# RWKV-5 attention and channel mixing on one core: decay weights as one row, second weight matrix in one burst, and a new order of the start

## The chip, the cores and the metric

The kernel runs on one core of one Trainium2 chip. The metric is the device time of one execution in microseconds (us). A profile is one execution recorded by the hardware profiler; its span runs from the first to the last instruction. Engines are named as in the profile: PE is TensorE (PEld its weight loads), DVE is VectorE, ACT is ScalarE, POOL is GpSimd, SP is SyncE, which here only issues DMAs.

## The reference

Inputs `r`, `k`, `v` have shape (4, 8, 768, 48): batch, heads, tokens, head dimension. Each head carries a 48x48 state through the tokens; the channel mixing that follows works on all 384 channels of a token.

```python
for t in range(S):
    cur = einsum('bhd,bhe->bhde', u[None] * kt, vt)
    y[:, :, t] = einsum('bhd,bhde->bhe', rt, state + cur)
    state = w[None, :, :, None] * state + einsum('bhd,bhe->bhde', kt, vt)
...
x = y.transpose(0, 2, 1, 3).reshape(4, 768, 384)
xn = (x - mean(x)) / sqrt(var(x) + 1e-06) * g_ln
out = x + maximum(xn @ w_ch1, 0.0) @ w_ch2      # w_ch1 (384, 1536), w_ch2 (1536, 384)
```

The term with `u` is the current-token term: for each token and head it is a number, the sum over the head dimension of r·u·k, times v.

## The kernel before

The tokens of each batch are cut into 6 chunks of 128, which makes 24 chunks, numbered 0 to 23; chunks 0, 6, 12 and 18 start with an empty state. Inside a chunk the recurrence is written as matrix products. With the position p of a token in its chunk, r is multiplied by w^p (step `SR`, giving `scr`) and k by w^-(p+1) (`SK`, giving `sck`); the factors `Fr` and `Fk` are made once, as exponentials of the logarithm of w (`LN`, `FR`, `FK`). Then, per chunk i:

- `LK`, `LR`, `LV` load k, r, v (192 KB each, in pieces of 192 bytes; ten buffers each). `CV` casts v to bf16.
- `TR` transposes scr and sck on PE into PSUM, `TC` (or its halves `TCr`, `TCk`) copies them out to `trs`. For chunks of the list K_BY_DMA two DMA transposes on SP do this instead (`TRD`, `TKD`).
- `AT` multiplies the transposed k and r into scores, `AM` masks them on DVE. `S` makes the chunk's addition to the state; `ZU` and `ZD` make the decayed state `Z` of it. `Y` is masked scores times v, plus r times the state of the chunk before.
- The current-token number per head is `cc`. For most early chunks it is made on PE: `Q` multiplies the transposed r and k, four small matmuls inside `S` sum them with u·w, and `CC` copies the result out. For chunks of the list CC_BY_DVE, `KU` and `KR` multiply k by u·w and by r, and `CC` is a sum on DVE. `VB` on POOL is v times cc.
- `X` adds Y and VB and gives the sum for the mean; `SQ` the squares; `XN` centres the row; `RS` makes the inverse deviation.

Channel mixing runs over groups of one or two chunks (GROUPS). `LT` and `XT` (or the DMA transpose `LTD`) transpose xn; `UP` is the product with w_ch1 into one of two PSUM banks named `hp`, twelve matmuls for a group of one chunk, six of double width for a group of two; `RL` is the relu out of `hp` into `hT`; `DN`, three steps of four matmuls per chunk, is the product with w_ch2; `OT` scales it, adds x, and `STO` stores. `UP,16*g+m` is part m of group g; `DN,4*i+d` is part d of chunk i.

The weight w_ch1 is loaded in three blocks of 768 KB each on SP (`LW1,n`) and cast to bf16 with the factor -g_ln in nine steps (`SW,3n` to `SW,3n+2`; `g_neg`). For a group of one chunk, UP part m needs block n = m. The weight w_ch2 is loaded in three blocks by DMAs that POOL issues and that cast to bf16 on the way (`IW2`; the page calls the queue q0, software_dynamic). `WU` and `DU` are matmuls of zeros that keep PE busy.

Nothing is scheduled by a program at build time: PLAN lists the steps in order, each with an index and an engine (v DVE, s ACT, g POOL), and every engine executes its own in that order. So an instruction that waits holds back all that stands behind it on its engine. SP issues its loads and stores one after another, and a full queue holds SP.

Steps and lines used below: `WF` L219, `LN` L267, `CL` L286 and its helper L281, `UR` L295, `FK` L307, `FR` L310, `LW1` L330, `SW` L332, `IW2` L344, `LK` L347, `LR` L350, `LV` L353, `TR` L369, `AT` L403, `S` L429 with L434, L441 and L448, `Y` L481 and L489, `LTD`, `TKD`, `TRD` L524, L528, L532, `LT` L537, `UP` L552, `RL` L568 and L570, `DN` L580. L204, L206 and L209 are helpers for copies and products.

Of the kernel before, what the change touches and what calls it, by code (L numbers as in the profile page):

```python
# [10 lines left out]
ACT = mybir.ActivationFunctionType  # L11
ENG = mybir.EngineType

GROUPS = [1, 1, 1, 1, 1, 1, 2, 2, 2, 2, 2, 2, 2, 2, 1, 1]
ZPE = [1, 2, 3]
K_BY_DMA = [16, 17, 18, 19, 20, 21, 22, 23]
CC_BY_DVE = [10, 11, 12, 13, 14, 15, 16, 17, 18, 19, 20, 21, 22, 23]
W_ROWS = True
SLOTS = {'kf': 10, 'rf': 10, 'vf': 10, 'sck': 3, 'scr': 3, 'vv': 4, 'trs': 3, 'q': 2, 'A': 2, 'cc': 4, 'ku': 2, 'kr': 2, 'Z': 3, 'ZS': 2, 'Vb': 3, 'x': 13, 'xn': 3, 'xT': 4, 'hT': 4, 'ot': 3}
PLAN = """  # L20
MW,0,v WF,0,- TL,0,s MI,0,g MP,0,v WU,13,- MM,0,g LK,0,- LN,0,s LR,0,- RI,0,s DU,10,-
CL,0,- FR,0,s LW1,2,- FK,0,s SR,0,v SK,0,v DU,12,- TR,0,- WL,0,s LR,1,- LV,0,- UR,0,g
LK,1,- TCk,0,s DU,18,- CU,0,- SR,1,g CV,0,s TCr,0,v LK,2,- SK,1,v AT,0,- LR,2,- UW,0,s
Q,0,v UGC,0,s TR,1,- SW,6,s SW,8,v LV,1,- SW,7,v S,0,- AMa,0,v CC,0,s LV,2,- TCk,1,s
SK,2,g AMb,0,v TCr,1,s LW1,0,- DU,16,- Y,0,- CV,1,s ZU,0,v CV,2,s SR,2,g DU,6,- AT,1,-
Q,1,v VB,0,g DU,5,- TR,2,- AMa,1,v S,1,- TC,2,s AMb,1,v IW2,0,g LW1,1,- IW2,1,g X,0,v
CC,1,s SW,1,s Q,2,v DU,13,- AT,2,- IW2,2,g XN,0,v Y,1,- SW,0,s AM,2,v SW,2,g LT,0,-
SQ,0,s LR,3,- XT,0,v VB,1,g ZU,1,v DU,15,- UP,2,- X,1,v S,2,- RL,2,s SW,3,v SW,5,v
XN,1,s DU,1,- UP,0,- CC,2,v SR,3,v SW,4,s VB,2,g LT,1,- LK,3,- DU,1,- Y,2,- RL,0,s
UP,1,- XT,1,s RS,0,g LV,3,- ZU,2,v UP,18,- SK,3,v SQ,1,s LR,4,- DN,0,- RL,1,s X,2,v  # L30
TR,3,- RS,1,g LK,4,- RL,18,s UP,16,- TC,3,v XN,2,s CV,3,v AT,3,- RL,16,s Q,3,v UP,17,-
SR,4,v SQ,2,s SK,4,g AM,3,v LT,2,- S,3,- RS,2,g LK,5,- XT,2,v Y,3,- TR,4,- CC,3,v
RL,17,s LV,4,- UP,32,- VB,3,g TC,4,s DN,1,- LR,5,- X,3,v RL,32,s UP,34,- Q,4,v XN,3,s
LK,6,- SK,5,v AT,4,- ZU,3,v RL,34,s LT,3,- UP,33,- AM,4,v XT,3,s SQ,3,s CV,4,g UP,50,-
RL,33,s SR,5,v RS,3,g S,4,- RL,50,s Y,4,- CC,4,v TR,5,- ZU,4,v LR,6,- VB,4,g UP,48,-
TC,5,s SK,6,v DN,2,- ZD,4,g LV,6,- X,4,v AT,5,- OT,0,v LV,5,- UP,49,- SQ,4,s Q,5,v
XN,4,s DN,4,- SR,6,v RS,4,g LK,7,- RL,49,s LT,4,- S,5,- DN,5,- XT,4,s CC,5,v LUB,0,-
CV,6,g AM,5,v TR,6,- CV,5,g LR,7,- DN,6,- RL,48,s VB,5,g LK,8,- Y,5,- SK,7,v TC,6,s
UP,64,- UWR,0,g X,5,v LV,12,- UP,66,- XN,5,s Q,6,v SR,7,g AT,6,- RL,64,s LV,7,- OT,1,v
LT,5,- SQ,5,s S,6,- DN,8,- XT,5,v SK,8,g LR,9,- CC,6,v AM,6,v RL,66,s TR,7,- RS,5,g  # L40
UP,81,- LR,8,- ZU,6,v UP,80,- VB,6,g TC,7,v LR,10,- DN,9,- RL,81,s SR,9,g Q,7,v LK,9,-
AT,7,- CV,7,s Y,6,- SR,8,g DN,10,- RL,80,s X,6,v LV,8,- UP,82,- OT,2,v SQ,6,s LK,10,-
S,7,- AM,7,v XN,6,s SR,10,g DN,12,- CC,7,s RL,82,s LR,12,- LT,6,- DN,13,- VB,7,g ZU,7,v
CV,8,s XT,6,v Y,7,- STO,0,- ZD,7,g TR,8,- LK,11,- X,7,v DN,14,- SK,10,g TC,8,v XN,7,s
UP,65,- LV,10,- Q,8,v SK,9,g LT,7,- AT,8,- RL,65,s LK,12,- XT,7,v S,8,- KU,10,v SQ,7,s
UP,96,- SK,11,g OT,3,v LV,9,- CC,8,s TR,9,- AM,8,v UP,101,- VB,8,g TC,9,s LR,11,- DN,16,-
ZU,8,v RS,6,g RL,96,s STO,1,- Y,8,- Q,9,v CV,9,s DN,17,- ZD,8,g LK,16,- X,8,v CV,12,s
S,9,- RL,101,s KR,10,v AT,9,- LK,14,- CC,9,s XN,8,s SK,12,v TR,10,- VB,9,g SQ,8,s AM,9,v
UP,99,- LR,20,- TC,10,s DN,18,- SR,11,g ZU,9,v LV,11,- UP,97,- CV,10,s CC,10,v ZD,9,g RL,99,s
AT,10,- OT,4,v STO,2,- RL,97,s S,10,- KU,12,v LT,8,- LK,13,- DN,20,- XT,8,s ZU,10,v SR,12,g  # L50
CV,11,s Y,9,- AM,10,v STO,3,- DN,21,- VB,10,g LV,13,- TR,11,- X,9,v ZD,10,g DN,22,- TC,11,s
LR,13,- KU,11,v Y,10,- SK,13,g UP,100,- OT,5,v SQ,9,s LK,15,- KR,11,v AT,11,- XN,9,s DN,24,-
LR,15,- SK,14,v RL,100,s KU,13,g X,10,v LT,9,- UP,98,- LR,16,- XT,9,s SR,13,v CV,13,s S,12,-
TR,12,- CC,11,v RL,98,s LV,14,- UP,114,- AM,11,v RS,7,g TC,12,s UP,117,- LK,21,- VB,11,g ZU,12,v
SQ,10,s Y,11,- KR,13,v TR,13,- LR,14,- XN,10,g X,11,v RL,114,s AT,12,- KR,12,v S,13,- RL,117,s
STO,5,- SK,15,v UP,112,- TC,13,s AM,12,v STO,4,- UP,113,- LK,19,- XN,11,s DN,25,- SK,16,g KU,14,v
RL,112,s LR,22,- LT,10,- DN,26,- XT,10,s SR,16,v UP,115,- LK,22,- SQ,11,s SR,14,v OT,6,v Y,12,-
RL,113,s TR,14,- RS,8,g LK,18,- CC,12,v RL,115,s DN,28,- TC,14,s AT,13,- LK,17,- KU,15,v SR,15,v
DN,29,- VB,12,g ZU,13,v LR,17,- TR,15,- AM,13,v UP,116,- ZD,13,g TC,15,s LV,15,- DN,30,- X,12,v
CV,14,g RL,116,s AT,14,- LR,23,- CC,13,v SQ,12,s Y,13,- OT,7,v LT,11,- STO,6,- S,14,- XN,12,g  # L60
DN,32,- XT,11,s KR,14,v LV,18,- VB,13,g LT,12,- KU,16,v UP,132,- TKD,16,- SK,17,g UP,131,- X,13,v
RL,132,s AM,14,v DN,33,- CV,15,s SR,17,g RL,131,s LV,16,- UP,130,- XN,13,s KR,15,v DN,34,- ZU,14,v
XT,12,s LR,18,- RL,130,s KU,17,v Y,14,- ZD,14,g OT,8,v S,15,- LR,19,- AT,15,- CV,18,v SQ,13,s
DN,36,- SK,18,g ZU,15,v STO,7,- UP,129,- CC,14,v LV,20,- ZD,15,g LT,13,- DN,37,- RL,129,v XT,13,s
LV,23,- UP,128,- KR,16,v SR,18,g AM,15,v DN,38,- TRD,16,- RL,128,s UP,133,- CV,16,s VB,14,g OT,9,v
S,16,- TRD,17,- KU,18,v UP,144,- RL,133,s RS,9,g ZU,16,v DN,40,- X,14,v SK,19,g LV,17,- CC,16,v
DN,41,- SQ,14,s UP,145,- SR,19,v LV,19,- DN,42,- CC,15,v VB,16,g RL,144,v XN,14,s LK,20,- Y,15,-
AT,16,- KR,18,v RL,145,s VB,15,g OT,10,v UP,147,- STO,8,- CV,19,s AM,16,v KR,17,g DN,44,- STO,9,-
UP,149,- CV,17,g X,15,v TKD,17,- ZD,16,g DN,45,- RL,147,v Y,16,- RL,149,v KU,19,g UP,148,- X,16,v
CV,20,s STO,10,- LT,14,- XN,15,s CC,18,v SR,20,g DN,46,- XT,14,v SQ,15,s LV,22,- RL,148,v AT,17,-  # L70
SQ,16,s S,18,- OT,11,v LT,15,- UP,146,- TKD,18,- SK,20,g CC,17,v XT,15,s DN,48,- RL,146,s RS,10,g
UP,163,- TKD,19,- AM,17,v DN,49,- VB,18,g RL,163,s UP,164,- ZU,18,v TRD,18,- XN,16,s VB,17,g KR,19,v
DN,50,- RL,164,s KU,20,g Y,17,- LK,23,- OT,12,v UP,160,- SK,21,g X,17,v DN,52,- TRD,19,- RL,160,s
KR,20,v AT,18,- KU,21,g CC,20,v DN,53,- LTD,16,- S,19,- SR,22,g DN,54,- AM,18,v XN,17,s UP,162,-
LR,21,- SQ,17,s SK,22,g OT,13,v UP,161,- RL,162,s CC,19,v AT,19,- KU,22,g LTD,17,- ZU,19,v UP,165,-
RL,161,s AM,19,v S,20,- RS,11,g DN,56,- TRD,20,- Y,18,- ZD,19,g RL,165,s UP,177,- X,18,v UP,181,-
TKD,20,- SR,21,g SQ,18,s Y,19,- RL,177,s DN,57,- VB,19,g KR,21,v STO,11,- UP,179,- SK,23,g STO,12,-
RL,181,s X,19,v DN,58,- ZU,20,v RL,179,s LV,21,- XN,18,g CC,21,v UP,180,- SQ,19,s SR,23,g TRD,21,-
XN,19,s UP,176,- OT,14,v RL,180,s AT,20,- CV,21,v RS,12,g DN,60,- LTD,18,- AM,20,v S,21,- DN,61,-
KU,23,g CV,23,v LTD,19,- Y,20,- ZD,20,g DN,62,- RL,176,v UP,178,- TKD,21,- OT,15,v VB,21,g UP,197,-  # L80
ZU,21,v VB,20,g RL,178,v DN,64,- TKD,22,- ZD,21,g AT,21,- X,20,v UP,193,- AM,21,v CV,22,g STO,13,-
SQ,20,s DN,65,- KR,23,g TRD,23,- RL,193,s S,22,- DN,66,- RL,197,s KR,22,g Y,21,- TRD,22,- UP,192,-
OT,16,v XN,20,g CC,22,v UP,194,- RL,192,s ZU,22,v VB,22,g STO,15,- DN,68,- X,21,v STO,14,- CC,23,v
AT,22,- SQ,21,s DN,69,- STO,16,- VB,23,g AM,22,v RL,194,s UP,195,- LTD,20,- RS,13,g XN,21,s DN,70,-
ZD,22,g UP,196,- TKD,23,- RL,195,s OT,17,v Y,22,- DN,72,- LTD,21,- AT,23,- X,22,v DN,73,- RL,196,s
XN,22,v STO,17,- SQ,22,s UP,210,- DN,74,- RS,14,g RL,210,s UP,212,- OT,18,v UP,209,- DN,76,- RL,212,s
LTD,22,- RL,209,s DN,77,- UP,208,- STO,18,- DN,78,- RL,208,s UP,211,- OT,19,v UP,213,- AM,23,v RL,211,s
DN,80,- RL,213,s DN,81,- STO,19,- DN,82,- Y,23,- OT,20,v UP,224,- DN,84,- X,23,v RL,224,s DN,85,-
XN,23,v STO,20,- DN,86,- SQ,23,s UP,226,- RS,15,g OT,21,v LTD,23,- UP,225,- RL,226,s DN,88,- RL,225,s
UP,240,- STO,21,- DN,89,- RL,240,s DN,90,- UP,241,- UP,242,- OT,22,v RL,241,s DA,0,- RL,242,s DA,1,-  # L90
DA,2,- DB,0,- STO,22,- OA,23,v DB,1,- DB,2,- OB,23,v SA,23,- SB,23,-
"""


@with_exitstack
def kernel(
    ctx: ExitStack,
    tc: tile.TileContext,
    r: bass.AP,
# [36 lines left out]
    group_of = {}  # L136
    for g, size in enumerate(GROUPS):
        for j in range(size):
# [545 lines left out]
```

## Time and profile before

| | |
|---|---|
| seven runs | median 156.38 us, 154.71 to 156.91 |
| the profiled execution | 156.68 us, span 154.6 us |
| PE busy | 144.2 us, 93% of the span |
| DVE, POOL, ACT busy | 110.1, 96.8, 89.0 us |
| mean granted PE clock | 0.975 |
| one UP step in the dense part, group of one / of two chunks | 0.67 / 0.655 us |
| one DN step (4 matmuls) | 0.65 us |
| AT / TR (scr and sck) / LT | 0.33 / 0.45 / 0.17 us |

The time of an execution is about 2.1 us longer than the span that its profile shows. Durations of the last three rows are distances between starts in the chain of work that ended last; single matmuls in the page's groups are longer, because matmuls overlap. A busy PE in the first 15 us is partly matmuls of zeros.

### The profile page before, as it was taken

Reading aid. Unit: us, or ns where it says so; the run is one execution under the profiler, and the core shown is the slowest. Engines: PE = TensorE matmul, PEld = TensorE weight load, DVE = VectorE, ACT = ScalarE, POOL = GpSimd, SP = SyncE. Lnnn points to the kernel's source line nnn. Section 1 sums busy time; section 2 is a strip of 40 time slices with the busy share of each in tenths; the row PEclk is TensorE's granted clock in tenths of the full one; section 3 lists DMA queues with packets and bytes.
Section 4 is the critical chain, followed back from the end, with each engine's and each line's share of the span. In section 5 each row is a group of like instructions: output and inputs, shape, how many; then the busy total and the mean of one; then the engine's idle time right before and its main releaser. Section 6 shows DMA issues by size and latency. Waiting matters only on the chain.

```text
span 154.6 us, 4487 instructions
## 1 busy us (share of the span) xinstructions
PE 144.2 (93%) x1788; PEld 117.3 (76%) x1788; DVE 110.1 (71%) x225; ACT 89.0 (58%) x186; POOL 96.8 (63%) x133
## 2 busy tenths in 40 slices
PE   7798975599999999999999999999999999999992
PEld 6697864488878788779877787777887777887881
DVE  2229950777989789999999789998877976335112
ACT  3536395148776658969966754376455147443440
POOL 3056636043799999998288598999899976100100
PEclk9999999559999999999999999999999999999998
DMA  4997999998999999989989978976472555212311
GB/s 70 288 233 137 303 260 207 199 194 167 183 184 203 205 220 193 246 171 211 244 162 223 227 149 193 230 77 139 100 203 53 134 156 140 77 55 79 99 55 51
DMA packets 92456, 25.98 MB, mean 168 GB/s; under 512 B 87442, under 2 KB 90900, under 8 KB 92436
## 3 DMA queue, kind: packets, MB, share of 16 engines
q1 hardware_dynamic: 92000, 24.52, 72.8%
q0 software_dynamic: 432, 1.18, 3.9%
q8 instruction: 14, 0.23, 0.6%
q14 instruction: 6, 0.05, 0.1%
q10 hardware_dynamic: 4, 0.00, 0.0%
HBM read 19.27 MB, written 4.72 MB: 155 GB/s over the span
## 4 chain that ended last, share of the span: by engine, by line
PE 79%; SPq 9%; DMA 9%; DVE 1%; issue 1%
PE hp L552 30%; PE o L580 29%; DMA rf<-in_r_dram 9%; PE at L403 5%; PE tr L369 4%; PE y L489 3%; SPq L353 3%; SPq L347 2%; PE s L448 2%; SPq L330 2%; PE y L481 2%; PE tr L537 2%; SPq L350 1%; PE o L595 1%; PE hp L595 1%
## 5 line engine op out<-in xcount | busy, mean ns | idle before, releaser
L552 PE MATMUL hp<-xT,w_sb 128*128 128x128 bf16 (+1 forms) x576 | 58.4, 250 | 0.3 <-DVE xT L206 0.2
L580 PE MATMUL o<-w_sb,hT 128*128 128x384 bf16 x276 | 55.0, 326 | 0.0
L552 PEld LDWEIGHTS <-w_sb 128*128 128x128 bf16 x576 | 49.1, 116 | 4.3 <-issue 0.5
L568 ACT ACTIVATE hT<-hp 128x512 bf16<-128x512 f32 x65 | 37.9, 595 | 22.4 <-PE hp L552 21.9
L580 PEld LDWEIGHTS <-hT 128*128 128x128 bf16 x276 | 24.8, 98 | 11.1 <-issue 0.2
L413 DVE TENSOR_TENSOR A<-at,mask 128x1024 bf16<-128x1024 f32 (+1 forms) x26 | 29.3, 1133 | 0.9 <-PE at L403 0.7
L636 DVE SCALAR_TENSOR_TENSOR ot<-o,rs,x 128x384 f32<-128x384 f32 x23 | 14.1, 612 | 16.2 <-PE o L580 14.5
L471 POOL TENSOR_TENSOR Vb<-vf,cc 128x384 f32<-128x384 f32 x24 | 21.1, 883 | 5.0 <-DVE cc L206 3.1
L209 POOL TENSOR_TENSOR sck<-kf,Fk 128x384 bf16<-128x384 f32 x15 | 16.1, 1080 | 11.3 <-PE at L403 6.0
L503 ACT ACTIVATE sqj<-x,sm 128x384 bf16<-128x384 f32 x24 | 14.7, 614 | 10.4 <-DVE x L496 10.3
L496 DVE SCALAR_TENSOR_TENSOR x<-y,Vb 128x384 f32<-128x384 f32 x24 | 13.2, 549 | 4.7 <-PE y L489 2.4
L204 ACT COPY trs<-tr 128x1024 bf16<-128x1024 bf16 (+1 forms) x14 | 12.8, 924 | 6.3 <-PE tr L369 6.3
L517 POOL TENSOR_SCALAR rs<-sq 128x1 f32<-128x1 f32 (+1 forms) x16 | 3.8, 236 | 18.6 <-ACT sqj L503 17.7
L209 POOL TENSOR_TENSOR scr<-rf,Fr 128x384 bf16<-128x384 f32 x14 | 14.6, 1047 | 0.8 <-DMA rf<-in_r_dram 0.8
L509 ACT ACTIVATE xn<-x,sm 128x384 bf16<-128x384 f32 x17 | 10.4, 613 | 6.5 <-DVE x L496 6.5
L209 POOL TENSOR_TENSOR Z<-ZS,WLZ 128x384 bf16<-128x384 f32 x13 | 13.4, 1032 | 1.1 <-DVE ZS L465 1.0
L209 DVE TENSOR_TENSOR scr<-rf,Fr 128x384 bf16<-128x384 f32 x10 | 5.7, 574 | 8.9 <-DMA rf<-in_r_dram 4.8
L262 PE MATMUL o<-warm 128*128 128x128 bf16 x110 | 10.6, 264 | 1.0 <-DVE warm L227 1.0
L204 ACT CAST vv<-vf 128x384 bf16<-128x384 f32 x14 | 7.1, 513 | 6.6 <-DMA vf<-in_v_dram 4.2
L520 POOL TENSOR_TENSOR rs<-rs,expo 128x1 f32<-128x1 f32 (+1 forms) x16 | 10.0, 625 | 1.3
L403 PE MATMUL at<-trs 48*128 48x128 bf16 x192 | 9.8, 222 | 0.1
L262 PEld LDWEIGHTS <-warm 128*128 128x128 bf16 x110 | 8.9, 122 | 1.1 <-DVE warm L227 1.0
(81 smaller groups left out, 190.0 us busy)
## 6 DMA issues: line engine op xcount, KB each, us to landing
kf<-in_k_dram SPq DMA_DIRECT2D x24, 192.0 KB, 4.1
rf<-in_r_dram SPq DMA_DIRECT2D x24, 192.0 KB, 4.3
vf<-in_v_dram SPq DMA_DIRECT2D x24, 192.0 KB, 4.1
out_dram<-ot SPq DMA_DIRECT2D x23, 192.0 KB, 2.8
w_f<-in_moe_w_ch_dram SPq DMA_DIRECT2D x3, 768.0 KB, 7.1
w_sb<-in_moe_w_ch_dram POOLq DMA_DIRECT2D x3, 384.0 KB, 8.8
w_b<-in_w_dram SPq DMA_DIRECT2D x1, 192.0 KB, 3.7
u_b<-in_u_dram SPq DMA_DIRECT2D x1, 192.0 KB, 4.5
```

What stands on the lines that cost most here:

```text
L204: nc.scalar.copy(out=out, in_=in_)
L209: engines[e].tensor_tensor(out=out, in0=in0, in1=in1, op=ALU.mult)
L262: nc.tensor.matmul(out=warm_ps[0][:, :P], lhsT=warm[:], rhs=warm[:], start=True, stop=True)
L403: nc.tensor.matmul(out=t[:, par, q, :], lhsT=trs(i)[p0 : p0 + D, 1, q, :], rhs=trs(i)[p0 : p0 + D, 0, q, :], start=True, stop=True,)
L413: nc.vector.tensor_tensor(out=AA(i)[:, a:b].rearrange("p e q t -> p (e q) t"), in0=psum["at", i][:, a:b].rearrange("p e q t -> p (e q) t") ...
L471: nc.gpsimd.tensor_tensor(out=Vb(i)[:].rearrange("p (h d) -> p h d", h=H), in0=vf(i)[:], in1=cc(i)[:].unsqueeze(2).to_broadcast([P, H, D]) ...
L496: nc.vector.scalar_tensor_tensor(out=xx(i)[:], in0=psum["y", i][:, :C], scalar=1.0, in1=Vb(i)[:], op0=ALU.mult, op1=ALU.add, accum_out=sm[ ...
L503: nc.scalar.activation(out=sqj[:], in_=xx(i)[:], func=ACT.Square, bias=sm[i][:], scale=-float(C), accum_out=sq[g][:, j : j + 1])
L552: nc.tensor.matmul(out=t[:, a * gw : (a + 1) * gw], lhsT=w1_sb[n][kc][:, fb::FB], rhs=xT(g)[:, kc, :gw], start=(kc == 0), stop=(kc == CK - 1),
L568: nc.scalar.activation(out=o, in_=s, func=ACT.Relu)
L580: nc.tensor.matmul(out=psum["o", i][:, :C], lhsT=hT(g)[:, fk, j * P : (j + 1) * P], rhs=w2_sb[d][:, a, :], start=(fk == 0), stop=(fk == FK ...
L636: nc.vector.scalar_tensor_tensor(out=ot(i)[:], in0=psum["o", i][:, :C], scalar=rs[g][:, j : j + 1], in1=xx(i)[:], op0=ALU.mult, op1=ALU.add,)
```

## The change

The functions stay as they are; five constants and PLAN are new.

```diff
-GROUPS = [1, 1, 1, 1, 1, 1, 2, 2, 2, 2, 2, 2, 2, 2, 1, 1]
+GROUPS = [1, 1, 1, 1, 1, 1, 1, 1, 2, 2, 2, 2, 2, 2, 2, 1, 1]
-K_BY_DMA = [16, 17, 18, 19, 20, 21, 22, 23]
-CC_BY_DVE = [10, 11, 12, 13, 14, 15, 16, 17, 18, 19, 20, 21, 22, 23]
-W_ROWS = True
+K_BY_DMA = [15, 16, 17, 18, 19, 20, 21, 22, 23]
+CC_BY_DVE = [12, 13, 14, 15, 16, 17, 18, 19, 20, 21, 22, 23]
+W_ROWS = False
```

With W_ROWS false, `WF` loads w as one row of 1.5 KB instead of 128 equal rows, `LN` takes the logarithm of one row, and a new step `WBM` spreads it to 128 rows by a matmul in float32 (1x128 ones by 1x384), from whose PSUM bank `FK` and `FR` read. The 128 rows of w that the current-token term on DVE needs come later by a new load, `LWB`.

```python
def WBM(i, e):
    t = psum["wb"] = ps.tile([P, 512], FP32, name="y")
    nc.tensor.matmul(out=t[:, :C], lhsT=ones[:], rhs=ln_b[:], start=True, stop=True)
def LWB(i, e):
    nc.sync.dma_start(out=w_b[:], in_=row_src(w, P))
```

PLAN is written anew throughout. The start of the SP queue, and what stands around the w_ch2 loads on POOL:

```diff
 SP
-WF LK0 LR0 LW1,2 LR1 LV0 LK1 LK2 LR2 LV1 LV2 LW1,0 LW1,1 LR3 LK3 LV3 LR4 LK4 LK5 LV4 LR5
+WF LK0 LR0 LR1 LK1 LV1 LV0 LK2 LR2 LV2 LR3 LW1,1 LK3 LW1,0 LR4 LV3 LK4 LW1,2 LV4 LK5 LR5
 POOL
-UR SR1 SK2 SR2 VB0 IW2,0 IW2,1 IW2,2 SW2 VB1
+UR SK1 SK2 VB0 SR2 SR3 XN0 IW2,0 IW2,1 IW2,2 VB1 RS0 XN1 SW2 VB2
 PE, behind S0 (matmuls of zeros: DU and how many)
-DU16 Y0 DU6 AT1 DU5 TR2 S1 DU13 AT2 Y1 LT0 DU15 UP2 S2 DU1 UP0 LT1 DU1 Y2 UP1 UP18 DN0 TR3
-UP16 AT3 UP17 LT2 S3 Y3 TR4 UP32
+DU16 AT1 DU5 Y0 S1 DU3 TR2 DU1 Y1 DU1 AT2 LT0 DU1 S2 DU9 UP1 TR3 DU3 Y2 DU6 LT1 DU3 AT3 DU3
+UP17 DU4 UP0 UP16 LT2 Y3 DN0 UP32 TR4 UP33 S3 UP34 UP2
 ACT, around SW8
+SW1 RL17 SQ2 RL0 XT2 SW8 RL32 RL33
 SP, near the end
-LTD19 TKD21 TKD22 STO13 TRD23 TRD22 STO15 STO14
+LTD19 STO13 STO14 TRD22 LK22 LR23 STO15 LTD20
```

The matmuls of zeros fall from 110 to 77. Several element-wise steps change engine: relu on ACT 65 to 69 and on DVE 7 to 3; XN on ACT 17 to 8, on POOL 4 to 10, on DVE 3 to 6; KR on DVE 11 to 5, on POOL 3 to 7; `Q` 10 to 12 times on DVE.

## The prediction, made before the changed kernel ran

> **What bounds the kernel now.** I read the page's busy shares and slices first, then the chain that ended last in order of time, the stretches of 2 us around the place that the chain points to, and the queues that act there.
>
> ```profile
> PE 144.2 (93%) x1788; PEld 117.3 (76%) x1788; DVE 110.1 (71%) x225; ACT 89.0 (58%) x186; POOL 96.8 (63%) x133
> ...
> PE   7798975599999999999999999999999999999992
> ...
> PEclk9999999559999999999999999999999999999998
> ```
>
> PE is full from the tenth slice on; no other engine is near that over the span. Two slices have half the clock. The chain says why:
>
> ```profile
> 14.22 0.49 SPq L330
> 14.75 13.19 DMA rf<-in_r_dram
> 27.96 0.56 DVE scr L209
> 28.52 0.23 DVE Z L209
> 28.91 0.56 DVE sck L209
> 29.51 0.61 PE tr L369 x4
> ```
>
> Until 14.7 us the chain is SP issuing loads, then r of chunk 3 (LR3, 13.19 us to landing), then PE to the end. The stretches (PE and PEld busy, DVE, ACT, POOL, granted clock, DMA share, GB/s):
>
> ```profile
> 18.00:20.00 2.00, 1.79 (x34) 1.67 (x30) 1.82 (x3) 0.57 (x1) 0.56 (x2) 1.00 0.99 371
> 22.00:24.00 2.00, 1.59 (x31) 1.52 (x32) 0.95 (x3) 2.00 (x5) 0.74 (x1) 1.00 1.09 204
> 26.00:28.00 2.00, 0.00 (x0) 0.00 (x0) 0.04 (x1) 0.00 (x0) 0.00 (x0) 0.87 1.16 228
> ```
>
> (28 to 34 us has a clock of 0.50.) And the issues, from the timeline of POOL and SP:
>
> ```profile
> 16.23 1.85 POOL L344 DMA_DIRECT2D w_sb<-in_moe_w_ch_dram  x3
> ```
>
> ```profile
> 13.43 1.27 SPq L330 DMA_DIRECT2D w_f<-in_moe_w_ch_dram  x2
> 14.75 0.49 SPq L350 DMA_DIRECT2D rf<-in_r_dram  x1
> 17.57 7.03 SPq L353 DMA_DIRECT2D vf<-in_v_dram  x1
> ```
>
> LR3 stands behind two w_ch1 blocks. These landed at 19.4 (ACT stopped waiting) and 14.2 + 8.0 = 22.2. The three w_ch2 pieces landed 7.6, 8.8 and 10.4 us after their issue: 23.9, 25.8, 27.9. r, k and v of chunk 3 landed at 27.95, 28.7, 29.5, only after the last of w_ch2. So while w_ch2 moves, about 5.8 us, the SP queue gets next to nothing through. PE stood 3.24 + 0.33 us for chunk 3, and the clock was halved from 27.4 to 34.3.
>
> **What the hole costs.** PE resumed at 28.58 and made its last matmul at 151.63. In the 5.7 us to 34.3 half was lost, 2.8 us. So from TR3 on there were 151.63 - 28.58 - 2.8 = 120.2 us of PE work at full clock, with no idle of note. The 3.0 us of store behind it stay. The change can win only ahead of this.
>
> **The change: the start of the SP queue.** It puts chunks 0 to 2 and LR3 ahead of any w_ch1. I walk it by rows. LK0, issued at about 1.2 us, lands after the shortest time of a chunk load, 2.9 us, plus a little: 4.4 (5.3 now, behind 192 KB of w). Landings stood 0.95 apart (R1 9.35, V0 10.3), later 0.75 to 0.8 (14.2, 15.0, 15.75); I take 0.95. Nine more loads: LR3 at 13.0. One w_ch1 block is 2.8 us (19.4 to 22.2): LW1,1 15.8, LK3 16.7, LW1,0 19.5, LR4 20.5, LV3 21.4. LK4 and LW1,2 come next.
>
> **w_ch2 on POOL.** Its issue now waits for XN0, so for X0 (16.71 us now). V0 lands 1.5 us earlier and DVE no longer scales LW1,2 ahead of X0 (0.88 us), so X0 falls between 14 and 16.7; I take 14.8, and with 0.6 for XN0 the issue is at 15.4 (16.2 now). The same 11.7 us to the last landing give 27.1. The first w_ch2 landing is then 23.1, less 1.9 for moving it: 21.2, about when LV3 (21.4) is through. So I let LV3 pass and LK4 not: LK4 about 27.3, LW1,2 about 2.4 later, 29.7. Bounds: 27.5 if LW1,2 shares with w_ch2, 31.5 if the 1.3 us gap in DMA traffic seen at 13 us comes again.
>
> **The new wait.** SW8 on ACT waits for LW1,2, and behind it stands RL32, which frees an `hp` bank; UP32 and UP33 fill both, so PE stops at UP34. SK4 on DVE waits for LK4, with SW6 and TC4 behind it. PE waits at TR4, then at UP34: landing + 0.72 (SW on ACT) + 0.6 (RL) + 0.1 = 29.7 + 1.4 = 31.1.
>
> By UP34 more is done than by TR3 before: TR3 and TR4 0.9, AT3 0.33, S3 0.44, Y3 0.37, LT2 0.17, two UP 1.34: 3.55 us. TR15 goes to DMA, -0.45. `S` sums the current-token number for chunks 10 and 11 again: one L434 group 0.1, twice +0.2. One group of two becomes two of one: 6 x 0.67 - 6 x 0.655 = +0.1. Left at UP34: 120.2 - 3.55 - 0.45 + 0.2 + 0.1 = 116.5. PE ends at 31.1 + 116.5 = 147.6, which is 4.0 less than 151.63; the span becomes 150.6, the time 156.68 - 4.0 = 152.7 us. The profiled execution is 0.3 above the median, so 152.5.
>
> **The clock.** Half clock came when PE had been idle for 2.1 us (25.3 to 27.4) and lasted until 34.3. The new wait at TR4 is about 2 us (UP32 ends near 26) with 1 to 2 more at UP34. No loss, or up to the same 2.8 us; I take none, since the wait is in two parts, and keep both ends. The Trainium skill, "TensorE: Matmul & The Clock Gate", Part 1, says that a free-running window of about 3.4 us decides; the two turns of the clock here lie 6.9 us apart, two windows, and by that rule the phase decides and the sum would be 152.5 or 155.3.
>
> **Dummies.** 77 in place of 110. They run where PE has no work, but they heat the clock: the first 23 took 2.64 us (115 ns each), 16 at 12.38 took 1.06 (66 ns), though the clock column prints 1.00 for both. With fewer, the fast state may come up to 3 us later; work ahead of 20 us would be late by at most half of that, 1.5 us, mostly inside the wait for LK4. I take 0.
>
> **w as one row.** Now w lands 3.7 us after issue at 4.42, then LN 0.52, FR, FK 0.6 each; TR0 at 7.00. A row of 1.5 KB is shown by no load on SP; between 1.6 us (the half stores) and 2.9. It saves 0.8 to 2.1. WBM costs 0.33 at least (L441, 384 columns bf16); the trace has no float32 product of this width, so up to the whole saving. Net 0 to -1.5 us at TR0, of which nothing reaches the end, as LK4 sets it. LWB adds 192 KB beside LUB, about 0.9 us of DMA ahead of chunk 9; PE waited for no load after 34 us.
>
> **The rest.** TRD15 and TKD15 hold SP for 2 x 1.25 us, with STO10, STO9 and LR17 behind; TC of 1.0 us goes from ACT. DVE loses KR 6 x 0.67, two sums 1.1 and relu 4 x 0.68, gains Q 2 x 0.53, TC 3 x 0.69 and XN 3 x 0.42: about -3 of 110. POOL gains XN 6 x 0.59, KR 4 x 0.95, loses SK, SR, UWR: about +4 of 97. ACT -8. All hide under a full PE; without cover each would cost its own size, 1 us. LK22 comes late, behind STO14 and TRD22: TRD 1.2, issue 0.6, landing 4.1, SK22 on POOL 1.0 are 7 us against some 8 us of PE work from DN65 to S22: between 0 and +2, I take 0.
>
> **The rivals.**
> *A, the clock falls in the new wait.* For it: 2 us idle were enough before. +2.8: 155.3.
> *B, w_ch2 gets ahead of chunk 3* (slower). The trace shows 4.3 us from its issue to the moment when the rate fell from 371 to 205 GB/s, and w_ch1 ran undisturbed until then. Should w_ch2 start at once, LW1,0, LR4 and LV3 fall behind it: V3 lands near 28.5, CV3 0.6, Y3 at 29.1; from Y3 there are 116.5 + 3.8 us (Y3, DN0, UP32, TR4, UP33, S3), and 2.8 for the clock: 152.2; with LW1,2 at 32.5 and two such waits, or the 1.3 us gap, 153.5: +1.9, 158.6. It decides when UP34 starts after 151.63 - 116.5 = 35.1. The Trainium skill, "DMA: Bandwidth & Descriptors", Queues, rings and completion order, says that a DMA engine takes turns between queues packet by packet; by that rule w_ch1 and w_ch2 share at once and the sum would be this rival's. The undisturbed 371 GB/s two to four us after the issue of w_ch2 speak against it, if its start is not merely late.
> *C, no wait at all*: w_ch2 issued late, LK4 and LW1,2 ahead of it; UP34 near 27.5: 149.0.
> *D, the hole merely moves* and the gain goes to a new stall late (LK22, POOL's order): 156.4.
>
> **How the numbers follow.** Forecast 0.43, A 0.17, B 0.17, C 0.13, D 0.10. The range reaches from C, 148.8, to 158.2, short of B's end. A measurement tells 1% (1.6 us) from no change. Faster: forecast, C and a third of A: 0.62. Same: the rest of A and D, a little of B: 0.21. Slower: most of B: 0.17.
>
> **What would show it.** Right: k of chunk 4 and w_ch1 block 2 land just after w_ch2, PE's longest wait is at TR4 or UP34 and at most 3 us, the clock stays at 1.00, and the last matmul is near 147.6. Wrong: PE waits for chunk 3 again; the clock is at 0.50 behind the wait (A); w_ch1 block 0 lands after 22 us (B); or PE idles behind 40 us (D).

## The result and the profile after

The changed kernel takes 158.21 us (median of 27 runs, 155.86 to 160.46); the kernel before takes 156.05 (64 runs beside them). The ratio is 1.0083, with a 95% interval of 1.0056 to 1.011. A second set gave 158.26 us and 1.017 [1.0086, 1.0253]. Each ratio here and below compares only those runs of the two kernels that lie within 1.5% of the fastest of their kernel, while the medians are of all runs, so a ratio need not be the quotient of two medians. So the change costs 0.8 to 1.7%, where 2.5% less was forecast. The profiled execution took 156.41 us, span 154.6. It is one of the shortest: the spans of 28 executions lie between 154.1 and 158.6, their median at 156.4.

The page of the changed kernel, busy shares, PE's slices and its clock:

```profile
PE 143.9 (93%) x1793; PEld 115.6 (75%) x1793; DVE 112.9 (73%) x221; ACT 83.7 (54%) x178; POOL 100.4 (65%) x142
...
PE   7999889799999999989999999999899979999990
...
PEclk9999999999999999999999999999999999999999
```

The two slices at half clock and the 5 and the 7 in front of them are gone: the start did what it was changed for. The 7 that stands at 27 to 31 us is the new wait of the forecast. New are 8 and 7 late, in slices that were all 9 before. The chain of waits (start, length, what):

```profile
18.21 10.78 DMA w_f<-in_moe_w_ch_dram
29.01 0.72 ACT w_sb L338
29.73 0.49 ACT hT L569
30.27 1.50 PE hp L553 x24
...
45.93 0.25 SPq L385
46.23 5.61 DMA u_b<-in_u_dram
51.94 0.56 DVE uw_b L210
```

The upper part is this new wait, in the order that the forecast gave: LW1,2 lands, SW8, RL32, UP34. In the kernel before, the chain from 29 us on was PE's own; here it leaves PE again at 46 us, for SP and the load of u. PE's timeline has all waits of 0.15 us and more from UP34 on (start, length, instruction, and in brackets the idle time before it and what ended it):

```profile
30.27 1.50 PE L553 MATMUL hp<-xT,w_sb 128*128 128x128 bf16 x24 [0.90 <-ACT hT L569]
...
54.48 0.40 PE L404 MATMUL at<-trs 48*128 48x128 bf16 x8 [0.69 <-DVE A L414]
...
63.91 0.37 PE L490 MATMUL y<-vv,A 128*128 128x48 bf16 x8 [0.15 <-DVE A L414]
...
68.60 0.34 PE L538 MATMUL tr<-ident,xn 128*128 128x128 bf16 x3 [0.75 <-DVE xn L512]
...
112.09 1.50 PE L553 MATMUL hp<-xT,w_sb 128*128 128x256 bf16 x12 [0.67 <-DMA xT<-xn]
...
124.56 0.81 PE L581 MATMUL o<-w_sb,hT 128*128 128x384 bf16 x4 [0.99 <-DVE ot L637]
```

Behind the start these are five waits, 3.25 us; the kernel before had none there. The profile of the second set has UP34 at 31.16 and 4.63 us in five waits, four of them on the same tiles, at 55, 69, 113 and 126 us. Four of the five in the list end with DVE. What DVE itself waited for, from its timeline:

```profile
51.94 0.56 DVE L210 TENSOR_TENSOR uw_b<-u_b,w_b 128x384 bf16<-128x384 f32 x1 [1.07 <-DMA u_b<-in_u_dram]
...
60.00 0.56 DVE L210 TENSOR_TENSOR scr<-rf,Fr 128x384 bf16<-128x384 f32 x1 [1.66 <-DMA rf<-in_r_dram]
...
123.89 0.62 DVE L637 SCALAR_TENSOR_TENSOR ot<-o,rs,x 128x384 f32<-128x384 f32 x1 [1.39 <-DMA out_dram<-ot]
```

Each is a transfer that came late, and all transfers but w_ch2's and two rows go through SP. Its timeline at two places:

```profile
33.56 1.41 SPq L351 DMA_DIRECT2D rf<-in_r_dram  x1
38.81 0.37 SPq L644 DMA_DIRECT2D out_dram<-ot  x1
...
45.54 0.65 SPq L385 DMA_DIRECT2D w_b<-in_w_dram  x1
46.23 0.43 SPq L382 DMA_DIRECT2D u_b<-in_u_dram  x1
...
113.56 2.53 SPq L533 DMA_TRANSPOSE trs<-scr  x2
116.20 1.19 SPq L525 DMA_TRANSPOSE xT<-xn  x1
117.48 1.22 SPq L529 DMA_TRANSPOSE trs<-sck  x1
118.79 1.21 SPq L525 DMA_TRANSPOSE xT<-xn  x1
120.05 1.05 SPq L644 DMA_DIRECT2D out_dram<-ot  x2
```

From 34.97 to 38.81 SP issues nothing. It stands at STO0, the store of chunk 0, which waits for OT0 on DVE (3.8 us, SP's longest wait), and the loads behind it stand too. In the second profile it stands there for 3.8 us as well; in the kernel before no store holds SP for more than 1.0 us between 30 and 120 us. Near the end five DMA transposes, 6.2 us of SP, go out one after another ahead of the store of chunk 13, whose buffer OT16 needs. What the first place does to the traffic, in stretches of 2 us of the changed kernel (the last two columns are DMA share and GB/s):

```profile
36.00:38.00 2.00, 2.00 (x32) 1.56 (x30) 1.46 (x4) 1.72 (x4) 1.81 (x4) 1.00 0.56 105
38.00:40.00 2.00, 2.00 (x33) 1.80 (x32) 2.00 (x4) 1.09 (x2) 1.92 (x4) 1.00 0.15 57
```

The kernel before moved 203 and 199 GB/s in the same two stretches.

### The profile page after: what moved, and what is told of

Its sections match the earlier page's. It is cut to its first block, busy times and chain, and to the rows that moved or that the text cites. A ratio compares the mean times of both kernels' runs of the same rounds, so it can differ in the third digit from the quotient of the medians.

```text
span 154.6 us, 4500 instructions
## 1 busy us (share of the span) xinstructions
PE 143.9 (93%) x1793; PEld 115.6 (75%) x1793; DVE 112.9 (73%) x221; ACT 83.7 (54%) x178; POOL 100.4 (65%) x142
## 3 DMA queue, kind: packets, MB, share of 16 engines
q0 software_dynamic: 432, 1.18, 4.0%
## 4 chain that ended last, share of the span: by engine, by line
PE 41%; DMA 21%; SPq 14%; DVE 12%; issue 5%; POOL 3%; ACT 1%; DVEq 0%; POOLq 0%; ACTq 0%
PE hp L553 17%; PE o L581 15%; DMA w_f<-in_moe_w_ch_dram 7%; SPq L348 4%; DMA u_b<-in_u_dram 4%; DMA rf<-in_r_dram 3%; SPq L354 3%; SPq L351 3%; DMA out_dram<-ot 2%; DMA vf<-in_v_dram 2%; DMA xT<-xn 2%; DVE ot L637 2%; SPq L331 2%; PE at L404 2%; PE tr L370 2%
## 5 line engine op out<-in xcount | busy, mean ns | idle before, releaser
L569 ACT ACTIVATE hT<-hp 128x512 bf16<-128x512 f32 x69 | 40.6, 594 | 33.0 <-PE hp L553 32.1
L553 PE MATMUL hp<-xT,w_sb 128*128 128x128 bf16 (+1 forms) x612 | 56.6, 241 | 1.8 <-ACT hT L569 0.9
L581 PE MATMUL o<-w_sb,hT 128*128 128x384 bf16 x276 | 53.2, 326 | 1.1 <-DVE ot L637 1.0
L210 POOL TENSOR_TENSOR sck<-kf,Fk 128x384 bf16<-128x384 f32 x13 | 13.9, 1067 | 7.5 <-DMA kf<-in_k_dram 4.0
L210 POOL TENSOR_TENSOR scr<-rf,Fr 128x384 bf16<-128x384 f32 x13 | 13.6, 1048 | 0.4 <-PE tr L370 0.4
L210 DVE TENSOR_TENSOR sck<-kf,Fk 128x384 bf16<-128x384 f32 x11 | 8.1, 742 | 4.9 <-ACT Fk L308 3.0
L205 ACT COPY trs<-tr 128x1024 bf16<-128x1024 bf16 x8 | 8.1, 1010 | 5.0 <-PE tr L370 4.8
L263 PE MATMUL o<-warm 128*128 128x128 bf16 x77 | 9.2, 274 | 1.0 <-DVE warm L228 1.0
L404 PEld LDWEIGHTS <-trs 48*128 48x128 bf16 x192 | 5.7, 97 | 5.6 <-issue 2.8
L490 PE MATMUL y<-vv,A 128*128 128x48 bf16 x192 | 8.9, 185 | 0.2 <-DVE A L414 0.2
```

The source lines that it names most:

```text
L205: nc.scalar.copy(out=out, in_=in_)
L210: engines[e].tensor_tensor(out=out, in0=in0, in1=in1, op=ALU.mult)
L404: nc.tensor.matmul(out=t[:, par, q, :], lhsT=trs(i)[p0 : p0 + D, 1, q, :], rhs=trs(i)[p0 : p0 + D, 0, q, :], start=True, stop=True,)
L553: nc.tensor.matmul(out=t[:, a * gw : (a + 1) * gw], lhsT=w1_sb[n][kc][:, fb::FB], rhs=xT(g)[:, kc, :gw], start=(kc == 0), stop=(kc == CK - 1),
L569: nc.scalar.activation(out=o, in_=s, func=ACT.Relu)
L581: nc.tensor.matmul(out=psum["o", i][:, :C], lhsT=hT(g)[:, fk, j * P : (j + 1) * P], rhs=w2_sb[d][:, a, :], start=(fk == 0), stop=(fk == FK ...
```

## The experiments

Theory 1: the start gained what was forecast, and the order behind it, SP's above all, gives it back. It has rivals: that an earlier start can't be carried to the end by any order; and that the late waits only stand for one another. Except where it is said otherwise, "waits" are PE's idle times of 0.15 us and more behind UP34 in the profile. Steps are named as in PLAN.

**The change again, and its two halves.** after_again is the changed kernel. start_only has its order up to UP18, rest_only has it from RL33 on, each with the order of the kernel before for the other part.

> The changed kernel once more, nothing edited, for a second profile and for its time beside the others of this group. Theory 1 (the start gained what was forecast, the later order gives it back in PE waits behind 30 us): UP34 starts at 30 to 31.5 us again, and PE idles 3 to 5 us behind it. Theory 2 (the first profile was a lucky one and the start itself is unstable): UP34 starts 2 us or more later, or the clock falls to 0.50 behind a wait ahead of 35 us. Ratio to before 1.005 to 1.015 under both.

> The changed order up to UP18 of chunk 1 (w as a row, w_ch2 in one burst, loads of chunks 0 to 2 first), then the order, groups and lists of before, with the 128 rows of w loaded just ahead of those of u. Theory 1: the gain of the start stays: 151.5 to 153 us, ratio 0.970 to 0.985, PE idle behind 31 us under 1 us. Theory 2: 155.5 to 158, ratio 0.995 or more. PE dense in both cases if no stall is in the order of before.

> The order of before up to the relu of UP33, then the order, groups and lists of after (128 rows of w from the start, so no spreading by TensorE and no second load of w). Theory 1: hole at 25 to 28 us as before plus the late waits of after: 158.5 to 160.5 us, ratio 1.015 to 1.03. Theory 2: the rest is as good as that of before: 155.5 to 157, ratio 0.995 to 1.005.

```diff
start_only: PLAN up to UP,18 from the changed kernel, the rest, GROUPS and lists from before; LWB ahead of LUB
rest_only:  PLAN up to RL,33 from before, the rest, GROUPS and lists from the changed kernel; no WBM, LWB
```

after_again came as theory 1 had it: UP34 at 31.16 and 4.63 us of waits. start_only gave 157.49 us, 1.0089 [1.0033, 1.0145]; rest_only 159.54, 1.0264 [1.0191, 1.0337]. rest_only speaks for theory 1: with the old hole in place (2.69 us at 28.9) the new order costs 2.6%, and PE has five late waits, 3.8 us. But for one on xn near 70 us they are not on the tiles that PE waited for in the changed kernel; three, 3.1 us, are on keys and r by DMA. start_only missed. UP34 came at 30.68, but at the joint XN3 stood behind RL18 on ACT, PE stood another 1.8 us near 35, and the clock was halved for 3.4 us. So it does not show the start alone.

**The start alone, cut later.**

> The changed kernel's order up to the second product of group 0's third up-projection block's successor (all of the start with its six groups of one chunk, w as one row, w2 issued behind w1), and from there the order, groups and lists of the kernel before; the row copies of w for the VectorE term are loaded just ahead of u. Theory 1 (the start gains what was forecast, the rewritten order behind it gives it back): UP34 starts at 30 to 31 us, PE waits behind it sum to under 1 us, span 150.5 to 152.5, ratio to the kernel before 0.965 to 0.985. Rival (the gain cannot be carried: a start that is earlier by 4 us meets the same loads later, so the waits come back wherever the order is): late waits of 2 us and more, ratio 0.99 to 1.01.

```diff
start_clean: as start_only, but the changed kernel's order up to DN,2 (XN3, RL18 and what follows them included)
```

157.09 us, 1.0134 [1.0052, 1.0216]: the forecast of theory 1 missed again, and its rival has a point. PE's waits, and the clock in stretches of 1 us:

```profile
30.65 2.72 PE L542 MATMUL hp<-xT,w_sb 128*128 128x128 bf16 x24 [0.83 <-ACT hT L558]
...
40.70 0.81 PE L570 MATMUL o<-w_sb,hT 128*128 128x384 bf16 x4 [0.71 <-DVE ot L626]
...
94.73 0.82 PE L542 MATMUL hp<-xT,w_sb 128*128 128x256 bf16 x6 [0.49 <-DVE hT L560]
...
95.78 0.81 PE L570 MATMUL o<-w_sb,hT 128*128 128x384 bf16 x4 [0.23 <-DVE ot L626]
```

```profile
30.00:31.00 1.00, 0.35 (x4) 0.39 (x5) 0.97 (x3) 1.00 (x4) 0.00 (x0) 0.79 1.01 195
31.00:32.00 1.00, 1.00 (x13) 1.00 (x11) 0.80 (x2) 0.14 (x2) 0.79 (x1) 0.50 1.11 206
...
33.00:34.00 1.00, 1.00 (x13) 0.57 (x11) 0.06 (x1) 0.60 (x2) 0.40 (x1) 0.51 1.01 196
```

The start is on time (UP34 at 30.65), but two things take the gain. The clock is at 0.50 for 3.4 us here, 1.7 us lost: PE was idle for 2.0 of the 4 us to 31, against 0.9 and 1.1 in the two profiles of the changed kernel. And the order of the kernel before, in which PE never waited late, now has four waits, 1.9 us together. At 94 to 96 us PE stands twice for DVE, which in the kernel before was busy for all of that stretch:

```profile
90.00:100.00 10.00, 9.99 (x104) 8.08 (x102) 10.00 (x20) 4.22 (x10) 9.21 (x12) 1.00 0.83 183
```

(Columns: length, PE, PEld, DVE, ACT, POOL, clock, DMA share, GB/s.) But DVE had itself just stood, for a DMA transpose of `scr`. DVE's wait in start_clean, the transposes on SP there, and the same ones in the kernel before:

```profile
92.91 0.71 DVE L199 TENSOR_TENSOR scr<-rf,Fr 128x384 bf16<-128x384 f32 x1 [0.61 <-DMA trs<-scr]
```

```profile
88.03 4.67 SPq L522 DMA_TRANSPOSE trs<-scr  x2
```

```profile
88.06 4.08 SPq L532 DMA_TRANSPOSE trs<-scr  x2
```

PE came to 94 us some 2 us ahead of the kernel before, but SP began these transposes no earlier. So the order before was just on time for the old start, and what the early PE meets here is SP's queue, by way of DVE.

**Is the dense part rigid?** In the kernel before, the score products of one chunk are repeated; the result is the same.

> The kernel before, with the score products of chunk 8 done seven times over (48 matmuls of about 41 ns more in one place near 55 us, some 2.0 us of TensorE; the result is the same). If TensorE's work behind the start is rigid, as the prediction's carried-over 120.2 us had it, all of it shows: ratio 1.011 to 1.014. Rival (elastic: in that stretch VectorE, GpSimd or the loads are nearly as late as TensorE, and a TensorE that is 2 us later or earlier meets them): under half shows, 0.999 to 1.006.

> The kernel before, with the score products of chunk 18 done seven times over (the same 2.0 us of TensorE near 110 us, behind most of the loads). Rigid: 1.011 to 1.014. Elastic up to the last chunks: under half, 0.999 to 1.006. Full here and little near 55 us would say that the give lies between the two places.

```diff
-        for q in range(HP):
+        for q in list(range(HP)) * (7 if i == 8 else 1):     # before_pe_late: i == 18
```

1.0176 [1.0104, 1.0247] and 1.0167 [1.0113, 1.0221]. The added work was sized too high: the 56 matmuls took 1.74 us where 8 take 0.40, so 1.34 us more, 0.9%. All of it shows, and more than it: nothing behind 55 us takes up a PE that is later. In the profile of before_pe_mid PE even has two new waits, 1.0 us together, on ot at 67 and on xT at 124 us. The profile of before_pe_late adds something by chance. Its hole was short (0.94 us), and ahead of the added work, which begins at 105.9, PE waits where it waited in start_clean:

```profile
94.49 0.82 PE L542 MATMUL hp<-xT,w_sb 128*128 128x256 bf16 x6 [0.60 <-DVE hT L560]
...
95.65 0.81 PE L570 MATMUL o<-w_sb,hT 128*128 128x384 bf16 x4 [0.34 <-DVE ot L626]
```

Here too DVE had just stood for a DMA transpose of `scr`, 0.72 us at 92.7. Later costs in full; earlier meets what was just on time. That this is SP's queue at 94 us is read from these profiles; no run moved the transposes in the old order.

**The store of chunk 0.**

> The changed kernel, with the store of chunk 0 moved on SP from ahead of five loads (v8, k7, r7, k9, v7) to behind them. In the profile of after SP sat from 35.0 to 38.8 us for that store's data, with the DMA share at 0.15 to 0.56. Theory 1a (that wait makes the loads of u and of r, chunk 11, late and so the PE waits at 54.5, 63.9 and 68.6 us): those waits, 1.6 us together, go, ratio to before falls by 0.008 to 0.012 against after. Rival (the waits come from the order on DVE, which would hold the same steps anyway): ratio unchanged within 0.003.

```diff
 SP
-LR10 STO0 LV8 LK7 LR7 LK9 LV7 LK11
+LR10 LV8 LK7 LR7 LK9 LV7 STO0 LK11
```

155.98 us, 0.996 [0.9903, 1.0018], 2.3 us less than the changed kernel by the medians of this set (2.1% by the ratios), about twice what theory 1a gave. The traffic in the two stretches:

```profile
36.00:38.00 2.00, 2.00 (x34) 1.62 (x32) 1.45 (x6) 1.93 (x4) 1.90 (x3) 1.00 1.11 218
38.00:40.00 2.00, 2.00 (x34) 1.81 (x32) 2.00 (x4) 0.89 (x2) 1.83 (x4) 1.00 0.86 168
```

The waits at 54, 64 and 125 us are gone, and so is DVE's wait for u. PE's wait on xn at 67 is still there (0.71 us), that on xT at 113 has grown to 1.21, and one of 0.93 us on the keys of chunk 15 (DMA) has come at 90. In all this profile has 3.48 us of waits, against 3.25 and 4.63 before the edit, so the waits do not show the whole gain in time. By the times, moving one store behind five loads on SP is the largest gain of the single mends that were tried.

**The buffers of ot.**

> The changed kernel with six ot buffers in place of three. Theory 1b (OT of chunk 16 waits for the store of chunk 13, which SP issues late; with six buffers it does not): the PE wait on ot at 124 to 126 us (0.99 and 1.60 us in two profiles) is gone, the others stay, ratio 0.007 to 0.012 under the changed kernel's, 0.998 to 1.006. Rival (that wait is only where a delay of VectorE shows; it turns up at the next xn or xT): no change, 1.008 to 1.017.

> The changed kernel with chunk 0's store moved behind the load of v of chunk 7 on SP, and six ot buffers. Theory 1: both effects add, the waits at 54, 64, 105 and 125 us are gone, what stays is the wait for xT at 113 us and some on trs, span 152.5 to 153.5, ratio 0.983 to 0.991. Rival (each late wait only covers the next one): as with the store moved alone, 0.993 to 1.0.

```diff
-'ot': 3
+'ot': 6          # sto0_ot6: and STO0 behind LV7
```

ot6 gave 157.67 us, 1.0136 [1.0037, 1.0235], no better than the changed kernel. Its wait at 125 us is gone, but the others sum to 4.75 us: 1.07 at 92 (keys by DMA) and 1.25 at 115 (xT by DMA) among them. The rival was right here: more buffers for ot take that wait away and bring nothing. That it is SP's lateness which came out there is the likely reading, not a tested one. sto0_ot6 gave 155.65, 0.9956 [0.9895, 1.0018], the same as with the store alone; its rival was right too.

**Chunk 15 by TensorE.** Its keys and r are turned by PE again, with a copy on ACT, on top of the two edits.

> The changed kernel with three edits against its late waits: chunk 0's store behind the load of v of chunk 7, six ot buffers, keys and r of chunk 15 by TensorE with a ScalarE copy. Theory 1 (the waits are made by SP's order and fall one by one): the wait for trs of chunk 15 (1.08 us) goes too, 0.7 us of TensorE work comes, span 152 to 153.5, ratio 0.983 to 0.992. Rival (elastic: a wait that is taken away turns up behind the next late engine): as with two edits, 0.993 to 1.0.

```diff
-K_BY_DMA = [15, 16, 17, 18, 19, 20, 21, 22, 23]
+K_BY_DMA = [16, 17, 18, 19, 20, 21, 22, 23]
 PLAN, with STO0 behind LV7 and six ot buffers
-TRD,15  TKD,15
+XT,12 TR,15,-   VB,16 TC,15,s
```

154.60 us, 0.9909 [0.9872, 0.9946]: faster than both kernels. This edit by itself, without the other two, was not measured. In sto0_ot6 SP was held at the turns of chunks 15 and 16, and PE waited for the keys of 15:

```profile
83.63 4.02 SPq L522 DMA_TRANSPOSE trs<-scr  x2
87.70 2.57 SPq L518 DMA_TRANSPOSE trs<-sck  x2
```

```profile
90.22 0.40 PE L393 MATMUL at<-trs 48*128 48x128 bf16 x8 [1.08 <-DMA trs<-sck]
```

SP held at two turns instead of four, in best1, and what is left of PE's waits:

```profile
84.02 1.35 SPq L522 DMA_TRANSPOSE trs<-scr  x1
85.46 1.83 SPq L518 DMA_TRANSPOSE trs<-sck  x1
```

```profile
30.67 1.50 PE L542 MATMUL hp<-xT,w_sb 128*128 128x128 bf16 x24 [0.89 <-ACT hT L558]
...
67.63 0.34 PE L527 MATMUL tr<-ident,xn 128*128 128x128 bf16 x3 [0.84 <-DVE xn L501]
...
90.23 0.33 PE L527 MATMUL tr<-ident,xn 128*128 128x128 bf16 x3 [0.28 <-ACT trs L194]
```

1.12 us where the two profiles of the changed kernel have 3.25 and 4.63. The larger wait that is left is again a load: XN9 stands on DVE behind the cast of v of chunk 11, and this cast waits for its load, which on SP stands behind k of chunk 12 and r of chunk 18. DVE's timeline:

```profile
66.88 0.37 DVE L196 CAST vv<-vf 128x384 bf16<-128x384 f32 x1 [1.44 <-DMA vf<-in_v_dram]
```

after_again and sto0_late have the same wait of DVE, 1.47 and 1.31 us. PE's last matmul ends at 148.69, so 148.69 - 30.67 - 1.12 = 116.9 us of work behind UP34; the forecast's 116.5 plus its 0.45 for chunk 15 on PE is 116.95.

**w as 128 rows again.**

> The changed kernel with w loaded as 128 rows at the start again (no spreading product on TensorE, no second load of w ahead of u). The prediction's step: first transposes at 7.0 us instead of 6.0, 0.9 us of DMA moved from 45 us to the start, UP34 as late or up to 0.5 us later, end within 0.5 us of the changed kernel's: ratio 1.006 to 1.018. Rival (the second load of w is what makes u_b late and VectorE wait 1.07 us at 52 us): that wait and TensorE's 0.69 us at 54 us go, ratio 1.000 to 1.005.

```diff
-W_ROWS = False
+W_ROWS = True          # WBM and LWB leave PLAN
```

158.83 us, 1.0102 [1.0027, 1.0177], as the changed kernel within the noise. TR0 starts at 7.11 us instead of 6.06, as the prediction's step had it. Whether that reaches the end its one profile, of its longest execution (160.22 us), can't tell: there PE waited 2.18 us for v of chunk 3 at 29.4, the clock was halved for 3.4 us, and UP34 came at 34.13, so the expectation for it missed. DVE's wait for u is gone without LWB, as it is with STO0 moved, which fits that u was late by both together; but here DVE also came to u 3.7 us later (54.6 against 50.9). In the total no difference is shown.

**What the start is worth.**

> The start of the kernel before up to the last up-projection of group 2's first column block (w as 128 rows, the hole at 28 us with its clock), and from there the changed kernel's order with the three edits (chunk 0's store later, six ot buffers, chunk 15 by TensorE). Theory 1 (the start is worth the 3.9 us that the prediction gave it, and the order behind it costs nothing once SP's order is mended): the time is that of the kernel with the new start and the three edits (0.9909) plus 3.0 to 4.0 us, ratio 1.010 to 1.018, late waits under 1.5 us in all. Rival (the later order was what had to be mended and the start is worth little): ratio 0.993 to 1.003.

```diff
rest_fixed: PLAN up to RL,33 from before, with its hole and w as 128 rows; the rest of best1
```

157.61 us, 1.0119 [1.0076, 1.0161]. Against best1's 0.9909 that is 2.1%, 3.3 us, for the start alone, w as one row included: the first half of theory 1 holds. Its second half, that the mended order costs nothing, does not. The same kernel against the kernel before differs in the order behind the start only, and there the new order still costs 1.2%; its profile has four waits behind 40 us, 0.34, 0.29, 0.28 and 0.89 us, together 1.8, which is 1.2% of the time. So the start's gain can be carried to the end, and in best1 the waits that were mended did not all come back: of the two rivals neither holds in full.

## Why the prediction was wrong

**The start: right where it counts.** The walk gave k of chunk 4 at 27.3, LW1,2 at 29.7 and UP34 at 31.1; the profiles show 26.9 (DVE's wait for it ends), 29.0, and UP34 at 30.27 and 31.16. w_ch2's issue came at 15.97 (15.4). The wait is where it was put, and in these two profiles rival B, w_ch2 ahead of chunk 3, did not happen. Rival C neither. But one step of the walk was a close call that falls either way. It had v of chunk 3 through at 21.4, just ahead of w_ch2, and in these two profiles it landed at 19.8 and 20.2. In those of start_only, sto0_late and ot6, with the same start, it landed at 26.0 to 26.3, together with the last of w_ch2, and PE waited for it up to 2.11 us (ot6). UP34 still came at 30.5 to 30.7 there, as LW1,2 set it. Two sums of the prediction are off, neither of which decides its forecast: rival B's work from Y3 to UP34 is 3.25 us by its own prices, not 3.8, and by its own walk V0 lands 1.15 us earlier, not 1.5.

**The clock: right for most executions.** It was full in the profile. One stretch of 3.4 us at half clock lowers the mean clock of a span of 155 us by 1.7/155, to 0.989; 6 of the 28 executions have that or less, against 17 of 23 of the kernel before beside the second set. Rival A is real: in start_clean 2.0 us idle in 4 halved the clock, and in the changed kernel 0.9 and 1.1 did not. The idle time alone does not decide, though: in the profile of ot6 PE was idle for 2.3 of the 3 us from 24 to 27, and the clock stayed at 1.00. The prediction took no loss "since the wait is in two parts"; in start_clean the idle time came in three pieces (1.18, 0.20 and 0.83 us), and the clock fell all the same. So that it stayed full in the changed kernel is in part luck. The Trainium skill, "TensorE: Matmul & The Clock Gate", Part 1, gives a free-running window of about 3.4 us; the length measured here, about 30.6 to 34.0, agrees. It names an idle window as what halves the clock; here PE had worked for half of the 4 us.

**The work behind UP34: right.** 116.5 us forecast, 116.96 in after_again, 116.9 (with chunk 15) in best1; 117.5 in the first profile. Waits below 0.15 us are counted as work in all of them.

**The step that failed:** "120.2 us of PE work at full clock, with no idle of note", carried over to an order that was new in every place. That order has waits. For after_again the sum closes: 0.06 (UP34) + 0.46 (work) + 4.63 (waits) = 5.15 us, and its last matmul ends at 152.75, 5.15 later than 147.6. A smaller term failed with it, "The 3.0 us of store behind it stay": from the last matmul to the end of the execution after_again took 5.5 us and the kernel before 5.05, and no view shows why. Together they make the 5.6 us between 152.7 and 158.28. The late waits are rival D, held at 0.10 and sought in LK22 and POOL's order. The largest part that an edit took away lies in SP's order from 35 us on, of which the prediction walked only the start and the end. Its own sentence "PE waited for no load after 34 us" was true of the kernel before and said nothing of the load stream after.

**"TRD15 and TKD15 hold SP":** named, with 2.5 us, and booked under a full PE. Taken out on top of the other edits they bring 0.9956 to 0.9909, a step whose intervals overlap; in the profiles the waits fall from 2.74 to 1.12 us, and the last matmul ends 1.6 us earlier though PE has 0.45 us more to do. The cover was gone, as PE waited for these very keys.

**LWB, "about 0.9 us of DMA ahead of chunk 9":** no cost in the total is shown, though it seems to have helped to delay u. **The engine moves:** POOL +3.6 us (forecast +4), ACT -5.3 (-8), DVE +2.8 (-3). DVE went the wrong way. The prediction took SK, SR and UWR off POOL but did not add them to DVE, where the rows of sck, scr and uw_b grew by 3.7 us (5.9 to 8.1, 5.7 to 6.6, none to 0.6). DVE is what PE waits for in four of the five places; no run here tells how much of that the added work caused.

**What stays open:** why the new order behind the start, mended, is still 1.2% behind the old one is only listed by its waits, not tested. The waits on xn at 67 us, behind the load of v of chunk 11, and on xT at 112 us, LTD behind the turns, were not tried by themselves.

## What to carry to other kernels

When a hole at the start is to be closed, the work behind it may be carried over only if its order is kept, and even then what is saved lasts only until the engine meets a queue or an engine that was just on time; a full engine's profile hides how near the others are. In an order written out by hand, follow the queue that all transfers share along its whole length: a store that waits for its result holds every load behind it, and showed here some 15 us later as another engine's wait. An engine that is waited for may itself be waiting: ask its own timeline before calling it the limit. Where a change does several things, mend its worst wait and keep its gain: three edits turned 1% slower into 0.9% faster.

## What the hardware showed unexpectedly

The spreading product in float32 (1x128 by 1x384) ran as two matmuls, 1.64 us together, where a bf16 matmul of 384 columns takes 0.33 (but later in the span; the 13 matmuls of zeros just ahead of it took 121 ns each, and 16 of them at 12.4 us in the kernel before 66 ns each); the row of w was used 1.3 us after its issue (issued at 0.73, LN at 2.03), below the lower bound of 1.6 that the stores gave.
